# Attention, a Fourier mix and an MLP on one core: where the raw weights' stores, the weight combinations and one activation table load stand in their queues

## The chip, the cores and the metric

The kernel runs on one core of a Trainium2 chip. The metric is the time of one execution on the device in microseconds (us), as the median over several runs. A profiled execution gives a trace: for every instruction its engine, its start and its length. TensorE (PE) multiplies matrices, VectorE (DVE), ScalarE (ACT) and GpSimd (POOL) work elementwise, and SyncE (SP) issues most of the DMA transfers. Each engine takes the instructions of its own queue in order.

## The reference

Eight batches of 576 tokens with 8 heads of 64 columns. The attention has no product of q with k: k is normalized by a softmax over the tokens, q by a softmax over a head's columns, and each head needs only a 64x64 product of k and v. What follows is a Fourier mix over tokens and columns, a layer norm, and an MLP 512 to 2048 to 512.

```python
q_s = np.exp(q - np.max(q, axis=-1, keepdims=True))
q_s = q_s / (np.sum(q_s, axis=-1, keepdims=True) + 1e-09)
k_s = np.exp(k - np.max(k, axis=2, keepdims=True))
k_s = k_s / (np.sum(k_s, axis=2, keepdims=True) + 1e-09)
kv = np.einsum('bhsd,bhse->bhde', k_s, v)
x = np.einsum('bhsd,bhde->bhse', q_s, kv)     # then (B, S, H*D): columns h*64+d
mixed = np.real(np.fft.fft(np.fft.fft(x, axis=1), axis=2))
u = x + mixed
un = (u - mean(u)) / np.sqrt(var(u) + 1e-06)  # over the last axis
out = u + np.maximum(un @ w_ch1, 0.0) @ w_ch2
```

The MLP's weights are handed over as 64-bit words: the core gets them as pairs of 32-bit integers and makes 32-bit floats of them itself.

## The kernel before, in words

**Groups and batches.** The MLP works on groups of 512 tokens. Groups 0 to 6 are the batches 0 to 6 without the 64 tokens of each that a Fourier symmetry folds differently; group 8 holds these tokens of all batches ("xs", "shared"); group 7 comes last. While one group's MLP fills PE, the attention, the transform and the norm of the next batch are interleaved with it, step by step. The order in which steps are written is a request: a scheduler below it arranges the instructions of each engine by priority and by what they wait for, and after that each queue is strictly in order.

**Attention.** `attention` makes items of a batch: 4 of k (two heads' columns each), 4 of q, and for even batches one of the folded tokens ("t"). Each item passes stages, pipelined one step apart: load (SP, L437 for k, L499 for q), exponential (DVE maximum, ACT exponential L457 for k, L521 for q, DVE sums up to L526), transposes on PE (L467, L532) with their copies on ACT (L468, into `ks`), and the matmuls with v (L484), whose result DVE scales into `kvr` (L487), or with kvr (L564).

**Fourier mix.** `transform` first folds x into sums and differences (`tokens_folded`, `columns_folded`, `by_frequency`, `columns_again`; tiles "eo", L603 to L625), one step each for batches from 1 on, then five blocks of small matmuls (L655, L658). `front` splits this into 9 steps for b > 0 with `late`, and `mix_own` (L678) follows with the second Fourier matrix and adds to x.

**Norm.** `norm` takes statistics of four tiles (`stats`), ACT the root (L730), DVE the reciprocal; `normal` scales on ACT (L744, groups from 1 on), `turn` transposes on PE (L750) and copies on ACT into `unT` (L754), and `combine` inside it forms the combinations of unT for Strassen (L348 to L351). ACT evaluates a function from a table set that must be loaded: the exponential and the root are in different sets, so the trace shows a load at the root (L730) and one at the next batch's first exponential (L457).

**The MLP.** Group 0 is multiplied plainly (`plain`): up has 16 steps f of 4 matmuls (L780) with a Relu (L782), down 64 steps in the order DOWN (L789, sum L794, then the store of the output; tiles of one half go by way of a buffer in DRAM, "mirror"). The groups after it use Strassen's scheme with 7 products of half-size blocks: up L850, down L886. Its 7 combinations of the weights come as a stream from DRAM (`w1s`, `w2s`) through four buffers in `big` (`load`, L384 to L395).

**Weights.** `round_blocks` fetches 32 blocks of words (L302 to L315, 512 KB each) into 11 places, and `convert` turns each into floats in `w1sb` and `w2sb`: ACT L329, DVE L330 and L331, ACT L334, POOL L335. A place that is free again takes a later fetch. During group 0's up, blocks up to 27 are converted; the last four, `rest`, follow during group 0's down. During that down, `combine(l, p)` also makes the combinations for layer l and pair p (POOL L341, DVE L343, for the second layer L348 to L351), and stores them beside the plain quarters from which they are made: L376 and L377 on SP store raw quarters, L379 to L382 the computed ones. `rest` and `combine` are one list, spread evenly over the first 60 of the 64 down steps:

```python
other = rest + combine
for i in range(len(down)):
    down[i]()
    for step in other[i * len(other) // 60:(i + 1) * len(other) // 60]:
        step()
```

The first three loads of the stream stand between the two layers' combinations, a fourth (18, which is pair 3's first-layer block) at their end.

**Holding.** `hold` takes the tiles in which batch 1's k and q will land, and `free(f)`, called after each up step f, gives them back by a tiny DVE copy that depends on the Relu of step f (k at f = 12, q at f = 14). That keeps batch 1's loads behind the words on the DMA engines. At f = 15 it copies one column of each of the 16 blocks of `w1sb` onto itself. Such a copy makes later readers of those columns wait for it: the first column of each block lies in the first half of its 512 columns, so the quarters 0 and 2 of the layer are concerned, and the odd quarters are not. The last k, v and q tiles of batch 1 land in the buffer of unT ("spare"), which is free when the last up matmul has read it.

Of the kernel before, what the change touches and what calls it, by code (L numbers as in the profile page):

```python
# [40 lines left out]
F32 = mybir.dt.float32  # L41
I32, U32 = mybir.dt.int32, mybir.dt.uint32
ACT = mybir.ActivationFunctionType
# [3 lines left out]
P = 128  # L47
# [5 lines left out]
HD = D // 2  # L53
# [9 lines left out]
NF = FF // P  # L63
# [59 lines left out]
class _Block:  # L123
# [129 lines left out]
    def hold(self):  # L253


        held = {12: [("k", S, 2)] * 2, 14: [("q", D, 3)] * 3}
        for f, some in held.items():
            for i, (tag, n, bufs) in enumerate(some):
                t = self.work.tile([P, n], F32, tag=tag, name=tag, bufs=bufs)
                self.nc.gpsimd.memset(t[0:1, 0:1], 0.0)  # L260
                some[i] = t[0:1, 0:1]

        def free(f):
            copy = self.nc.vector.tensor_copy
            for t in held.get(f, ()):
                copy(t, self.h0[0:1, f, 0:1])
            if f == NF - 1:
                copy(self.w1sb[0:1, :, 0:1], self.w1sb[0:1, :, 0:1])
        return free

    def shared(self, a, b):
# [318 lines left out]
    def transform(self, b):  # L590


        nc, V, G = self.nc, self.nc.vector, self.nc.gpsimd
        Z = self.work.tile([P, KT, HD], F32, tag="Z", name="Z", bufs=1)
        self.Z[b] = Z
        x = {(c, u): self.xpart(b, c, u) for c in range(2) for u in range(2)}
        eo = {}

        def tokens_folded(some=range(4)):
            for i in some:  # L600
                e, op = ((V if b == 0 else G), ALU.add) if i < 2 else (V, ALU.subtract)
                eo[i] = self.halves()
                e.tensor_tensor(out=eo[i][:, 0:D], in0=x[i % 2, 0], in1=x[i % 2, 1], op=op)  # L603

        def columns_folded(some=range(4)):
            for i in some:
                e, op = ((V if b == 0 else G), ALU.add) if i < 2 else (V, ALU.subtract)
                t = eo[i]
                e.tensor_tensor(out=t[:, 1:HD], in0=t[:, 1:HD], in1=t[:, D - 1:HD:-1], op=op)
                if b == 0:  # L610
                    self.warm(t[:, 0:HD], 2)

        def by_frequency(some=range(4)):

            for i in some:
                e, op = ((G, ALU.add), (G, ALU.subtract), (V, ALU.add), (V, ALU.subtract))[i]
                one, two = eo[i // 2 * 2], eo[i // 2 * 2 + 1]
                (V if b == 0 else e).tensor_tensor(out=eo[i][:, NN:], in0=one[:, 0:NN], in1=two[:, 0:NN], op=op)

        def columns_again(some=(2, 3, 0, 1)):  # L620

            for i in some:
                t, y = eo[i], eo[i][:, NN:]
                V.tensor_tensor(out=t[:, 0:QD], in0=y[:, 0:QD], in1=y[:, HD:QD:-1], op=ALU.subtract)
                V.tensor_tensor(out=y[:, 0:QD], in0=y[:, 0:QD], in1=y[:, HD:QD:-1], op=ALU.add)  # L625

        def at_first():

            for some in ((2, 3), (0, 1)):
                for f in (tokens_folded, columns_folded, by_frequency, columns_again):  # L630
                    f(some)

            t = self.small.tile([P, 1], F32, tag="root", name="root", bufs=1)
            V.tensor_scalar(out=t[:], in0=eo[1][:, NN:NN + 1], scalar1=0.0, scalar2=None, op0=ALU.mult)
            nc.scalar.activation(t[:], t[:], ACT.Sqrt)
            self.wait_for(eo[1][:, NN:], [self.raws[i] for i in range(4)])

        def block(k):


            g = self.live["g", b]
            sines = k in (2, 3)
            own = slice(*{0: (NN, NN + QD), 4: (NN + QD, NN + QD + 1), 1: (0, QD), 2: (NN + 1, NN + QD + 1),
                          3: (1, QD)}[k])
            tail = slice(*{0: (0, QD), 4: (QD, QD + 1), 1: (NN, NN + QD), 2: (1, QD + 1), 3: (NN + 1, NN + QD)}[k])
            n = own.stop - own.start
            if k == KT:

                own, tail = slice(own.start, own.start + P), slice(tail.start, tail.start + P)
            full = self.acc((own.stop - own.start, 512))  # L650
            pz = full[0:n]
            f = sines * NM
            for odd, at, size in ((1, 0, MO), (0, MO, ME)):
                t = eo[3 - odd if sines else odd]
                nc.tensor.matmul(full[:, at:at + size], lhsT=t[:, own], rhs=self.ft[:, f + at:f + at + size], start=at == 0,  # L655
                                 stop=False, skip_group_check=True)
            f += 2 * NM
            nc.tensor.matmul(full[:, 0:NM], lhsT=g[:, tail], rhs=self.ft[:, f:f + NM], start=False, stop=True,  # L658
                             skip_group_check=True)
            z, zt = (self.Zr[0:1], self.ZTr[0:1]) if k == KT else (Z[0:n, k, :], self.ZT[0:n, k, :])  # L660
            nc.scalar.copy(paired(z), interleaved(pz[:, NT - 1:NT - 1 + 2 * ME])[:, 0:P, :])

            at = W * (b % 2)
            nc.scalar.mul(paired(zt[:, at:at + Q]), interleaved(pz[:, 0:2 * MO])[:, 0:NT - 1, ::-1],
                          -1.0 if sines else 1.0)
            nc.scalar.copy(paired(zt[:, at + Q:at + W]), interleaved(pz[:, 0:2 * ME])[:, NT - 2::-1, ::-1])

        folds = [tokens_folded, columns_folded, by_frequency, columns_again] if b else [at_first]
        return folds + [lambda k=k: block(k) for k in (2, 3, 0, 1, 4)]

    def second(self, z, zr, add):

# [43 lines left out]
    def norm(self, g):  # L716

        nc, V = self.nc, self.nc.vector
# [9 lines left out]

        def scales(s):
            nc.scalar.activation(std[:, s], mv[:, s, 1], ACT.Sqrt, bias=self.eps[:, 0:1])  # L730
            V.reciprocal(std[:, s], std[:, s])
            V.scalar_tensor_tensor(out=mv[:, s, 0], in0=mv[:, s, 0], scalar=-1.0, in1=std[:, s], op0=ALU.mult,
                                   op1=ALU.mult)
# [211 lines left out]
def kernel(ctx: ExitStack, tc: tile.TileContext, q, kT, v, w1, w2, ft,  # L945
# [4 lines left out]
    def front(b, loads=None):  # L950

        first = blk.attention(b, loads)
        steps = late(lambda: blk.transform(b), 9 if b else 6)
        mixes = [lambda c=c: blk.mix_own(b, c) for c in range(2)]
        if b % 2:

            mixes.insert(0 if b == B - 1 else 2, lambda: blk.mix_shared(b // 2))
        return first, steps + mixes

    def late(make, n):  # L960

        box = []

        def run(i):
            if not box:
                box.extend(make())
            box[i]()

        return [lambda i=i: run(i) for i in range(n)]
# [33 lines left out]
    for order, g in enumerate(groups):  # L1003
        loads = [] if g == 0 else None
        one, two = front(order + 1, loads) if order + 1 < B else (blk.later, [])
        if g == 0:
            up, down = blk.plain(0, nexts.pop(0))

            round_blocks(range(4))
            n = 2 * NF - 8  # L1010
            for f in range(NF):
                up[f]()
                free(f)
                round_blocks(range(4 + n * f // NF, 4 + n * (f + 1) // NF))
            rest = [lambda i=i: round_blocks([i]) for i in range(4 + n, 2 * NF)]
            combine = [lambda l=l, p=p: blk.combine(l, p) for l in range(2) for p in range(NP)]
            combine[NP:NP] = [lambda i=i: blk.load(15 + i) for i in range(3)]
            combine.append(lambda: blk.load(18))
            for step in loads:
                step()  # L1020

            side = one + two + norm(1)
            gaps = [2] + [2] * 4 + [8] + [2] * (len(one) - 6) + [3] * 5 + [1] * 4 + [2] * (len(two) - 9) + [1] * 7
            other = rest + combine
            at = 0
            for i in range(len(down)):
                down[i]()
                for step in other[i * len(other) // 60:(i + 1) * len(other) // 60]:
                    step()
                while side and at + gaps[0] <= i:  # L1030
                    at += gaps.pop(0)
                    side.pop(0)()
            for step in side:
                step()
            continue

        jobs, down = blk.up(order, nexts.pop(g)), blk.down(g, order)

        merged(flat(jobs), one)
        merged(down, two + (norm(groups[order + 1]) if order < B else []))  # L1040
# [52 lines left out]
```

## Time and profile before

| what | value |
|---|---|
| median of 3 runs | 1142.52 us (1142.41 to 1143.66) |
| profiled execution, its own time | 1142.0 us |
| its span, first to last instruction | 1140.2 us |
| granted TensorE clock | 0.996 |
| DMA moved | 193.79 MB, mean 170 GB/s |
| ACT_TABLE_LOAD, each | 1.28 us |

The profile's page gives the busy time of each engine over the span, the span in 40 slices, and groups of instructions. A slice is 28.5 us here; the digits are tenths of busy time, and the row of GB/s is what the DMA engines moved:

```profile
PE   5899999989999999999999999999999999999997
...
DVE  6785756488324833384435643683344352203201
ACT  6495423274124513371226322641233142201200
...
DMA  9377784463346534554356436543453344444451
```

The first two slices are the attention of batch 0, while the words are still on their way; group 0's MLP takes slices 3 to 7, and from about 200 us on each group's Strassen products run with the next batch beside them.

Two more kinds of view are used below. A timeline lists one engine's instructions in the order of time: start and length in us, the engine, the line, the instruction with its tiles, and how many alike stand in a row; a square bracket at the end gives how long the engine had been idle and what released it. A table by stage gives, for each stretch of time, the length, then the busy us of PE, PE's weight loads, DVE, ACT and POOL (number of instructions in brackets), the clock, the share of DMA and GB/s.

### The profile page before, as it was taken

The numbers are of one execution on the slowest core, as the hardware profiler recorded it, in microseconds if no ns is written. First come the engines' busy times: TensorE is split into PE (matmuls) and PEld (weight loads), VectorE is DVE, ScalarE is ACT, GpSimd is POOL, SyncE is SP. The second block draws the span as 40 slices with busy tenths as digits, with TensorE's granted clock in tenths as the row PEclk, the third lists the DMA queues.
The fourth block names the chain that finished last, engine by engine and source line by source line (L and its number), as shares of the span: only waits on it lengthen the run. The fifth ranks groups of instructions, "written<-read, shape, count | busy, mean of one in ns | idle before, by whom it ended". The sixth has DMA issues, their size and how long they took to land.

```text
span 1140.2 us, 14639 instructions
## 1 busy us (share of the span) xinstructions
PE 1098.6 (96%) x5472; PEld 919.1 (81%) x5472; DVE 543.4 (48%) x1110; ACT 397.7 (35%) x956; POOL 332.5 (29%) x302
## 2 busy tenths in 40 slices
PE   5899999989999999999999999999999999999997
PEld 4644556878888988888889888888889888888886
DVE  6785756488324833384435643683344352203201
ACT  6495423274124513371226322641233142201200
POOL 2075541245012600324024402260034213302320
PEclk9999999999999999999999999999999999999999
DMA  9377784463346534554356436543453344444451
GB/s 310 120 258 243 258 279 148 149 213 140 122 150 206 202 111 143 183 195 154 124 176 213 148 113 190 195 172 107 143 191 148 114 163 148 185 139 154 150 185 55
DMA packets 92549, 193.79 MB, mean 170 GB/s; under 512 B 23088, under 2 KB 59696, under 8 KB 85312
## 3 DMA queue, kind: packets, MB, share of 16 engines
q1 hardware_dynamic: 90680, 191.82, 49.5%
q10 hardware_dynamic: 1800, 1.05, 0.3%
q8 instruction: 43, 0.70, 0.2%
q14 instruction: 26, 0.21, 0.1%
HBM read 168.72 MB, written 28.31 MB: 173 GB/s over the span
## 4 chain that ended last, share of the span: by engine, by line
PE 79%; DVE 11%; ACT 4%; DMA 2%; issue 2%; POOL 1%; SPq 0%; ACTq 0%; POOLq 0%; DVEq 0%
PE bb L850 14%; PE bb L886 13%; PE bc L886 10%; PE bc L850 9%; PE ba L850 9%; PE ba L886 8%; PE acc L484 3%; PE acc L564 2%; PE bc L789 2%; PE acc L655 2%; PE acc L658 2%; PE acc L678 1%; PE tr L750 1%; PE tr L532 1%; PE tr L467 1%
## 5 line engine op out<-in xcount | busy, mean ns | idle before, releaser
L850 PE MATMUL bb<-unT,big 128*128 128x256 f32 x768 | 187.9, 381 | 0.3 <-DVE u L822 0.3
L886 PE MATMUL bb<-big 128*128 128x256 f32 x768 | 172.8, 379 | 0.0
L850 PEld LDWEIGHTS bb<-unT,big 128*128 128x128 f32 x768 | 142.8, 190 | 23.8 <-DVE u L818 3.4
L886 PEld LDWEIGHTS bb<-big 128*128 128x128 f32 x768 | 145.1, 190 | 20.1
L341 POOL TENSOR_TENSOR big<-big 128x512 f32<-128x512 f32 (+1 forms) x38 | 45.1, 1187 | 309.5 <-ACT big L862 305.6
L850 PE MATMUL bc<-unT,big 128*128 128x256 f32 x512 | 125.3, 379 | 0.0
L850 PE MATMUL ba<-unT,big 128*128 128x256 f32 x512 | 124.3, 379 | 0.0
L862 ACT ACTIVATE big<-big 128x512 f32<-128x512 f32 x96 | 60.2, 628 | 171.3 <-DVE big L861 171.0
L886 PE MATMUL bc<-big 128*128 128x256 f32 x512 | 116.5, 379 | 0.5 <-DVE x L903 0.5
L886 PE MATMUL ba<-big 128*128 128x256 f32 x512 | 114.1, 379 | 0.0
L886 PEld LDWEIGHTS bc<-big 128*128 128x128 f32 x512 | 95.9, 190 | 14.1 <-DVE x L903 0.9
L886 PEld LDWEIGHTS ba<-big 128*128 128x128 f32 x512 | 95.9, 190 | 12.3
L850 PEld LDWEIGHTS bc<-unT,big 128*128 128x128 f32 x512 | 95.5, 190 | 12.5
L850 PEld LDWEIGHTS ba<-unT,big 128*128 128x128 f32 x512 | 95.0, 190 | 11.7
L822 DVE TENSOR_TENSOR u<-bb,s 128x512 f32<-128x512 f32 x40 | 27.6, 689 | 134.8 <-PE bb L886 79.1
L521 ACT ACTIVATE q<-q,qm 128x64 f32<-128x64 f32 x240 | 61.5, 337 | 10.2 <-DVE qm L519 9.4
L349 POOL TENSOR_TENSOR unT<-unT 128x512 f32<-128x512 f32 x8 | 14.2, 1773 | 172.9 <-DVE unT L348 172.9
L818 DVE TENSOR_TENSOR u<-bb,s 128x512 f32<-128x512 f32 x40 | 27.6, 690 | 76.8 <-PE bb L850 38.1
L898 POOL TENSOR_TENSOR x<-x,u 128x512 f32<-128x512 f32 x14 | 17.7, 1267 | 148.2 <-DVE u L822 118.0
L861 DVE TENSOR_TENSOR big<-bc,u 128x512 f32<-128x512 f32 x64 | 44.1, 688 | 26.1 <-PE bc L850 25.3
L814 ACT COPY s<-ba 128x512 f32<-128x512 f32 x40 | 23.4, 584 | 89.4 <-PE ba L886 45.5
L754 ACT COPY unT<-tr 128x512 f32<-128x512 f32 x36 | 20.6, 585 | 86.5 <-PE tr L750 86.0
(221 smaller groups left out, 1656.7 us busy)
## 6 DMA issues: line engine op xcount, KB each, us to landing
big<-w1s SPq DMA_DIRECT2D x64, 896.0 KB
big<-w2s SPq DMA_DIRECT2D x56, 1024.0 KB
big<-in_w_dram SPq DMA_DIRECT2D x21, 512.0 KB
k<-in_kT_dram SPq DMA_DIRECT2D x26, 288.0 KB
q<-in_q_dram SPq DMA_DIRECT2D x27, 256.0 KB
v<-in_v_dram SPq DMA_DIRECT2D x26, 256.0 KB
words<-in_w_dram SPq DMA_DIRECT2D x11, 512.0 KB
w2s<-big SPq DMA_DIRECT2D x8, 512.0 KB
```

Of the source, the lines that this page charges most:

```text
L341: e1.tensor_tensor(out=to(4), in0=at(2), in1=at(3), op=ALU.add)
L484: nc.tensor.matmul(pk, lhsT=ks[:, c, :], rhs=v[:, c, :], start=(c == 0), stop=(c == NC - 1))
L521: nc.scalar.activation(heads[:, h, :], heads[:, h, :], ACT.Exp, bias=m[:, h:h + 1])
L564: nc.tensor.matmul(px[:, r * P:(r + 1) * P], lhsT=qT[:, r, :], rhs=self.kvr[b % 2][:, r, :], start=True, stop=True)
L655: nc.tensor.matmul(full[:, at:at + size], lhsT=t[:, own], rhs=self.ft[:, f + at:f + at + size], start=at == 0, stop=False, skip_group_chec ...
L814: nc.scalar.copy(temp("s1"), box["ba"][:])
L818: V.tensor_tensor(out=temp("u2"), in0=box["bb"][:], in1=box["s1"][:], op=ALU.add)
L822: V.tensor_tensor(out=temp("u3"), in0=box["bb"][:], in1=box["s1"][:], op=ALU.add)
L850: nc.tensor.matmul(bank()[:, i, :], lhsT=w[:, WA_AT[m], k * P:(k + 1) * P], rhs=unT[:, B_AT[m], k, :], start=first and i == 0 and k == 0, ...
L861: V.tensor_tensor(out=hp(i), in0=bank[:], in1=u[:], op=ALU.add)
L862: nc.scalar.activation(hp(i), hp(i), ACT.Relu)
L886: nc.tensor.matmul(bank()[:, i, :], lhsT=h[p][:, A_AT[m], i * P:(i + 1) * P], rhs=w[:, p, :], start=first and i == 0 and p == 0, stop=p == ...
```

## The change

Four places are edited.

- `free` at f = 15 copies two strided views onto themselves: of all 16 blocks of `w1sb` the columns 0 and 256, and of the first 12 blocks of `w2sb` (blocks 16 to 27 of the words) the same two. So the odd quarters are concerned too, and so are the raw stores of the second layer that read these blocks.
- `rest` and `combine` are two lists: `rest` has one step at down steps 0, 3, 6 and 9, and `combine` is spread over the 50 down steps from 12 on.
- In `norm`, groups from 1 on get one exponential of a single column after the root, into a small tile of its own that nobody reads. It needs the exponential's table set, which is therefore loaded there.
- `transform` has one empty step between the folds and the blocks for batches from 2 on, and `front` asks for 10 steps there instead of 9.

```diff
@@ free
             if f == NF - 1:
-                copy(self.w1sb[0:1, :, 0:1], self.w1sb[0:1, :, 0:1])
+                for w in (self.w1sb[0:1, :, ::HD], self.w2sb[0:1, 0:NF - 4, ::HD]):
+                    copy(w, w)
@@ transform
-        return folds + [lambda k=k: block(k) for k in (2, 3, 0, 1, 4)]
+        return folds + [lambda: None] * (b > 1) + [lambda k=k: block(k) for k in (2, 3, 0, 1, 4)]
@@ norm, scales
             nc.scalar.activation(std[:, s], mv[:, s, 1], ACT.Sqrt, bias=self.eps[:, 0:1])
+            if g > 0:
+                t = self.small.tile([P, 1], F32, tag="root", name="root", bufs=1)
+                nc.scalar.activation(t[:], std[:, 0:1], ACT.Exp)
             V.reciprocal(std[:, s], std[:, s])
@@ front
-        steps = late(lambda: blk.transform(b), 9 if b else 6)
+        steps = late(lambda: blk.transform(b), (6, 9, 10)[min(b, 2)])
@@ group 0's down
-            other = rest + combine
             at = 0
             for i in range(len(down)):
                 down[i]()
-                for step in other[i * len(other) // 60:(i + 1) * len(other) // 60]:
+                for step in rest[i // 3:i // 3 + 1] if i % 3 == 0 else []:
+                    step()
+                j = max(0, i - 12)
+                for step in combine[j * len(combine) // 50:(j + 1) * len(combine) // 50 if i >= 12 else 0]:
                     step()
```

## Prediction

> **What bounds the kernel now.** I read the page first, then the stages, then every wait of the TensorE in order of time, then what the releasing engine did. The page says PE is busy 1098.6 of 1140.2 us, so all waits of PE together are 41.6 us, and only those that the change can reach are worth counting.
>
> ```profile
> PE 1098.6 (96%) x5472; PEld 919.1 (81%) x5472; DVE 543.4 (48%) x1110; ACT 397.7 (35%) x956; POOL 332.5 (29%) x302
> ```
>
> The stages show where they lie (the column after the length is PE busy): the first 60 us (about 21 us idle) and the end (8 us after 1100) are not touched; 100 to 150 has 4.2 us, 225 to 275 has 3.8 us.
>
> ```profile
> 100.00:125.00 25.00, 23.93 (x59) 10.62 (x59) 9.34 (x22) 9.03 (x16) 10.04 (x13) 1.00 0.78 248
> 125.00:150.00 25.00, 21.89 (x103) 14.13 (x104) 22.30 (x57) 15.60 (x49) 10.05 (x12) 1.00 0.78 295
> ...
> 225.00:250.00 25.00, 22.57 (x127) 18.83 (x125) 18.08 (x42) 17.74 (x50) 6.85 (x7) 1.00 0.51 166
> 250.00:275.00 25.00, 23.68 (x132) 20.83 (x131) 22.53 (x37) 16.57 (x50) 13.79 (x10) 1.00 0.49 191
> ```
>
> PE's timeline gives each wait (in brackets: us waited and the releaser). After 275 us there are only 3.8 us of them before the last stage.
>
> ```profile
> 99.97 3.67 PE L780 MATMUL bc<-unT,big 128*128 128x512 f32 x8 [0.94 <-ACT big L782]
> ...
> 126.63 1.38 PE L484 MATMUL acc<-v,ks 128*128 128x128 f32 x10 [2.69 <-ACT ks L468]
> ...
> 147.60 0.49 PE L564 MATMUL acc<-kvr,qT 128*128 128x128 f32 x2 [1.48 <-DVE kvr L487]
> ...
> 232.14 0.66 PE L467 MATMUL tr<-ident,k 128*128 128x128 f32 x4 [1.47 <-ACT k L457]
> ...
> 254.11 0.66 PE L532 MATMUL tr<-ident,q 128*128 128x128 f32 x4 [1.32 <-DVE q L526]
> ...
> 478.28 0.66 PE L467 MATMUL tr<-ident,k 128*128 128x128 f32 x4 [1.04 <-ACT k L457]
> 479.67 1.38 PE L484 MATMUL acc<-v,ks 128*128 128x128 f32 x10 [0.19 <-ACT ks L468]
> ```
>
> The pair at 478/479 returns at 721.96/723.35. ACT shows why: the table load stands between the last Relu and the first exponential, on the path.
>
> ```profile
> 476.06 1.28 ACT L457 ACT_TABLE_LOAD   x1
> 477.36 0.78 ACT L457 ACTIVATE k<-k,km 128x576 f32<-128x576 f32 x1
> ```
>
> The wait at 126.63 is a chain through SP's queue: k loads, ACT's exponentials of k, the Relu of f=14 behind them (114.60), the q loads that it frees, the spare loads behind those, their maximum on DVE (124.46) and exponential (125.24), and then the copy of ks that PE waits for.
>
> ```profile
> 100.62 1.81 SPq L377 DMA_DIRECT2D w2s<-big  x3
> ...
> 107.91 0.83 SPq L437 DMA_DIRECT2D k<-in_kT_dram  x2
> ...
> 115.38 2.73 SPq L499 DMA_DIRECT2D q<-in_q_dram  x3
> ...
> 118.67 0.39 SPq L437 DMA_DIRECT2D spare<-in_kT_dram  x1
> ```
>
> **What the Trainium skill says.** "ScalarE: Activation LUTs", What ACT_TABLE_LOAD costs: about 1283 ns for the load, plus a drain of about 1380 ns, for every switch of set. The load agrees (1283 ns, 7 times at L457 and 7 at L730); no drain is seen, the exponential starts 1.30 us after its load does. I use 1.28. "PSUM — Partial Sum Buffer", Engine vs sequencer instructions: ScalarE, VectorE and GpSimd queues are strict FIFO, and matmuls start in program order. The trace agrees: the Relu of f=14 (L782) stood behind two exponentials until 114.60. So the order of each queue decides, and I compared the orders of both kernels' instructions.
>
> **The change, part by part** (line numbers of before).
>
> *Raw stores held.* Before, 8 stores of the w1 quarter (L377, 128 KB) go out from 79.81, and w2's raw stores stand between the last word fetches. In the new order the w1 ones come after the spare loads, one ahead of each combination's; of w2's raw stores one pair stays between fetches 29 and 30, and 13 stand behind fetch 31 and ahead of the k loads. Two waits are new. First, DVE's 24-element copy on w2sb waits for POOL's conversion 25 (done 97.62); behind it on DVE are conversions 26 and 27, which ran from 95.35, so they start 2.3 us late, POOL's follow at 99.7 and 101.0 instead of 97.67 and 98.95, and fetches 30 and 31 go out at about 101.0 and 102.3 (before 98.99 and about 100.2). They then have less ahead of them, so I let them land as before. Second, 13 stores at 0.43 to 0.60 us each (L376 and L377 rows) need 5.6 to 7.8 us of SP, and the third from last waits for conversion 30: k loads at about 109 instead of 107.91. Passing that on with DMA's lighter backlog: Relu of f=14 +0.6, q loads +0.6, spare loads 119.3, their landing 124.4 instead of 123.8 (from the DMA semaphores in the trace). But before, DVE's maximum did not start at the landing: a combination waiting for POOL (L343) held it until 124.46. With that moved behind, the maximum starts at 124.4 again, so the end of the wait stays at 126.6. The 0.94 at 99.97 lies before it on PE; removed or not, it is made up in this wait. Sum: 0, from -1.0 to +1.5, with a tail taken up below.
>
> *Combinations behind the keys.* Up to the last kvr (L487, 146.97) DVE runs without a gap from 126.4. In the new order the same span holds as many half-size combinations (14), but conversion 30 (L330 and L331, 1.38 us) has moved ahead of it. Part is lost to waits for the stores, so the kvr comes 0.9 us earlier and the wait of 1.48 is 0.6: gain 0.9 (0 to 1.5). The combinations' DMA waits now stand on DVE ahead of q's sums; I traced the tightest (the store of pair 5's raw halves, out about 138.6, landing about 142, wanted at 145) and charge nothing; the cover is 3 us. Layer two's chain ends near 190 on POOL, wanted at 200; the load of pair 3 moves from 185 behind a mirror store that waits for the last down matmul (201.10): about 203, landing by 209, wanted at 214. Cover 5 us, charged 0.
>
> *Where the batch 1 transposes go.* Before, PE puts down matmuls between them:
>
> ```profile
> 198.88 0.60 PE L750 MATMUL tr<-ident,eo 128*128 128x128 f32 x4
> 199.32 1.02 PE L789 MATMUL bc<-big 128*128 128x512 f32 x2
> 200.18 0.60 PE L750 MATMUL tr<-ident,eo 128*128 128x128 f32 x4
> 200.62 1.89 PE L850 MATMUL ba<-unT,big 128*128 128x256 f32 x8
> ```
>
> In the new order all four tiles stand in a row at the end. With two banks and 0.58 us copies, working on: first transposes at 199.0, copies end at 200.2 and 200.7, the fourth normalization (queued behind them on ACT, 0.75) at 201.4, the third tile's copy at 201.95, and L850 starts then, not at 200.62: loss 1.35 (0.5 to 1.6).
>
> *Exponential table behind the root.* Each of 8 norms gets a load and one small exponential, 1.5 us, on ACT after the root; its normalizations are queued behind and start about 1.0 us later (before: root done 194.23, first one at 194.73). From batch 2 on the new order puts the first transpose up to 7 matmuls (3 us) later, which covers it; ACT is 35% busy. Seven loads leave the exponentials' path. At 478 and 722 the exponential moves 1.28 up, so 1.04 goes; but the matmul between transpose and L484 has moved behind L484, so of 0.19+0.43 about 0.62 is waited: gain 1.23-0.62=0.6 each, 1.2 together (0 to 2). At 232 the transpose itself stands two matmuls (0.86) earlier, so 1.47 becomes about 0.95: gain 0.5. The five transposes of q after it stand 3 to 12 matmuls later; of their waits (0.61+0.30+1.32=2.2) I take 1.6 (0.8 to 2.2).
>
> *The empty step.* For b>1 the blocks move one place down. First blocks of batch 7 stand 4 matmuls (1.7 us) later, so the 0.55 at 889.43 goes, and the transposes at 802.54 (0.39) stand 7 later: gain 0.9 (0.4 to 0.95).
>
> Sum: 0+0.9-1.35+1.2+0.5+1.6+0.9 = 3.75 us. The profiled execution: 1142.0, span 1140.2, 1.8 outside. So 1138.2 for it; the median of the runs shown is 0.5 above it: 1138.8.
>
> **Rivals.**
> A smaller gain: the kvr stays late and the q waits shift with the keys (0.9 and 1.6 gone, a little more lost at 200): 1141.2. For it: DVE is busy 22.3 of 25 us there, and its waits on stores are new. Against: the q transposes do move.
> A larger one: the held stores let the fetches land earlier, and both 0.94 and 2.69 go with the rest kept: 1135.8. For it: the DMA share is 0.78 there. Against: the spare loads cannot start before the first layer has read the buffer (117.2).
> Slower: the k loads are stuck behind w2's raw stores on SP. If fetch 30 and 31 take 6 us, as the third words fetch before did (91.7 to 98.1), instead of 3, conversion 30 is done near 111, and the stores behind it at 0.6 us push the k loads to about 116. Each us is then passed on through Relu, q and spare loads to PE: 7 us against 3.75 gained, near 1146. It decides from 6 us of delay (k loads at 115). For it: SP is in order and nothing else carries k. Against: fewer bytes stand ahead of them.
>
> **How the numbers follow.** A change counts here from 0.2% (2.3 us). Forecast 1138.8: 0.50; smaller 0.25; larger 0.08; slower 0.17. Faster: 0.48 of the first, 0.08, and 0.04 of the smaller: 0.60; same 0.23; slower 0.17. The parts' bounds give 1135.5 to 1142.5 for the first; to leave out no more than two in ten I reach to 1143.5.
>
> **What will show it.** k loads on SP near 109, spare's maximum near 124.4, L484's wait still near 2.7; kvr near 146; L850's first matmul about 1.3 us after the last transpose with a wait on ACT; no table load at L457 after batch 1, and waits at 478 and 722 on L484 instead of L467. I am wrong if k loads come after 112, if DVE waits for w1s stores between 137 and 147, or if L850 waits for the load of pair 3.

## The result, and the profile after

| | median | runs | ratio to before |
|---|---|---|---|
| before, beside the first runs of the change | 1143.09 us | 4 | |
| the change, first runs | 1144.22 us | 4 | 1.0004 (0.9983 to 1.0025) |
| before, beside the later runs | 1142.97 us | 43 | |
| the change again (e7 below) | 1142.51 us | 14 | 0.9996 (0.9986 to 1.0005) |

The change makes no difference that can be measured; the forecast of 1138.8 us was wrong. The profiled execution took 1142.6 us with a span of 1140.8 us at a clock of 0.995, against 1142.0, 1140.2 and 0.996 before.

To see where the time went, I compare the start of the same matmul of the MLP in both traces. The next table is worked out from the two records of PE; a shift above zero is later than before.

| place on PE (time before) | shift in the changed kernel, us | forecast for the stretch | measured for the stretch |
|---|---|---|---|
| group 0, first up matmul (61.0) | +0.15 | | |
| group 0, down matmul 49 (152.3) | +2.90 | -0.9 | +2.75 |
| group 1, first up matmul (200.6) | +4.11 | +1.35 | +1.21 |
| group 1, last up matmul (266.5) | +3.27 | -2.1 | -0.84 |
| group 5, last up matmul (754.0) | +2.53 | -1.2 | -0.74 |
| group 6, last down matmul (935.1); no change after it | +0.97 | -0.9 | -1.56 |

From 200 us on the forecast holds: 3.14 us come back where 4.2 were expected. The loss sits before 152 us. This is the timeline of PE in the changed kernel (start, length, instruction, and in brackets the wait and its releaser); the waits answer to those shown at 99.97, 126.63, 147.60, 478.28 and 479.67 of before:

```profile
103.41 3.67 PE L788 MATMUL ba<-unT,big 128*128 128x512 f32 x8 [0.80 <-ACT big L790]
...
119.28 3.70 PE L797 MATMUL bc<-big 128*128 128x512 f32 x8 [1.34 <-ACT big L790]
...
128.57 2.36 PE L487 MATMUL acc<-v,ks 128*128 128x128 f32 x10 [2.46 <-ACT ks L471]
...
150.50 0.49 PE L567 MATMUL acc<-kvr,qT 128*128 128x128 f32 x2 [0.79 <-DVE kvr L490]
...
203.04 0.66 PE L758 MATMUL tr<-ident,eo 128*128 128x128 f32 x4 [0.24 <-ACT unT L762]
204.24 0.66 PE L758 MATMUL tr<-ident,eo 128*128 128x128 f32 x4 [0.54 <-ACT eo L752]
...
481.89 1.38 PE L487 MATMUL acc<-v,ks 128*128 128x128 f32 x10 [0.62 <-ACT ks L471]
```

The four transposes in a row cost what was said, and the kvr wait (the one at 150.50) halved, though not for the reason given in the forecast, as the experiments show. But the first k times v (L487, L484 before) starts at 128.57, not at 126.6; a new wait of 1.34 on a Relu stands ahead of it. Its ten matmuls then take 2.36 us where they took 1.38. SP's queue shows the cause of the first, the clock that of the second.

SP's timeline (each line is what SP spent on issuing, waits included):

```profile
101.53 1.58 SPq L317 DMA_DIRECT2D words<-in_w_dram  x2
103.15 0.43 SPq L379 DMA_DIRECT2D w2s<-big  x1
...
111.61 0.47 SPq L379 DMA_DIRECT2D w2s<-big  x1
112.17 0.91 SPq L440 DMA_DIRECT2D k<-in_kT_dram  x2
119.43 2.57 SPq L502 DMA_DIRECT2D q<-in_q_dram  x3
...
122.57 0.38 SPq L440 DMA_DIRECT2D spare<-in_kT_dram  x1
```

The k loads go out 4.26 us later than before (107.91), and q and spare loads follow 4 us later. Even an empty SP could not have sent them before 110.5: the k tile is given back only after the Relu of f=12, and that one stood on ACT behind the conversion of late words:

```profile
108.67 0.68 ACT L337 ACTIVATE words<-words 128x512 int32<-128x512 uint32 x1 [1.40 <-DMA words<-in_w_dram]
109.24 0.58 ACT L790 ACTIVATE big<-bc 128x512 f32<-128x512 f32 x1
109.72 0.59 ACT L790 ACTIVATE big<-ba 128x512 f32<-128x512 f32 x1
```

The last of these three is the Relu of f=12; before it ran at 107.11, behind words that had landed by 105.89.

Of the 4.26 us only 1.94 reach the first k times v. The maximum of the spare tile on DVE, which it needs, no longer stands behind a combination that waits for POOL (first two lines, before); it starts as soon as its data have landed (last line, after):

```profile
123.61 0.93 DVE L343 TENSOR_TENSOR big<-big 128x256 f32<-128x256 f32 x1 [2.73 <-POOL big L341]
124.46 0.74 DVE L455 TENSOR_REDUCE km<-spare 128x1 f32<-128x576 f32 x1
...
126.39 0.75 DVE L458 TENSOR_REDUCE km<-spare 128x1 f32<-128x576 f32 x1 [4.13 <-DMA spare<-in_kT_dram]
```

The traces of the experiments below show two effects. In the eight kernels whose first layer's raw stores are not held, the maximum stands behind this combination, and from the k loads to the first k times v it takes 18.2 to 18.7 us (17.5 in e2). In the six that hold them, the maximum starts at the landing, and it takes 16.4 to 16.8 us (17.8 in e7). So the hold shortens this chain by about 2 us, but in the changed kernel the chain starts 4.26 us later.

The clock: two tables by stage, first the kernel before, then the changed one, cut on the grid of the trace's clock record, whose rate changes only there. After the length come PE's busy us; the third number from the end is the clock.

```profile
121.60:125.01 3.41, 2.33 (x10) 1.03 (x8) 1.40 (x2) 0.00 (x0) 2.66 (x4) 1.00 0.99 290
125.01:128.42 3.41, 1.79 (x16) 1.79 (x17) 2.46 (x8) 2.14 (x5) 0.00 (x0) 1.00 1.07 404
128.42:131.84 3.42, 3.42 (x22) 2.46 (x21) 3.36 (x8) 2.25 (x5) 1.34 (x1) 1.00 0.34 130
```

```profile
125.34:128.76 3.42, 0.96 (x3) 0.19 (x2) 1.07 (x3) 1.56 (x4) 2.12 (x3) 1.00 0.96 290
128.76:132.17 3.41, 3.41 (x16) 3.37 (x16) 1.38 (x4) 0.39 (x2) 0.72 (x1) 0.50 1.07 399
```

The changed kernel waits no longer there than the one before (2.46 against 2.69 us), but its wait falls almost whole into one stretch of 3.41 us, and the next stretch runs at half rate: half of 3.41, that is 1.7 us of work, is lost there, and the shift grows from 1.94 at the start of the first k times v to 3.59. Of this 0.69 comes back at the kvr wait, which PE now reaches later; 2.90 are left. Before, the wait was cut in two by the edge at 125.01, and nothing followed.

### The profile page after: what moved, and what is told of

It is laid out like the page before. It is cut to its first block, busy times and chain, and to the rows that moved or that the text cites. A ratio compares the mean times of both kernels' runs of the same rounds, so it can differ in the third digit from the quotient of the medians.

```text
span 1140.8 us, 14655 instructions
## 1 busy us (share of the span) xinstructions
PE 1099.8 (96%) x5472; PEld 920.9 (81%) x5472; DVE 536.1 (47%) x1111; ACT 403.1 (35%) x967; POOL 332.9 (29%) x302
## 4 chain that ended last, share of the span: by engine, by line
PE 84%; DVE 4%; issue 2%; DMA 1%; POOL 1%; ACT 1%; SPq 0%; POOLq 0%; DVEq 0%; ACTq 0%
PE bb L894 15%; PE bb L858 14%; PE bc L894 10%; PE ba L894 10%; PE bc L858 10%; PE ba L858 9%; PE acc L487 2%; PE acc L567 2%; PE bc L797 2%; PE acc L658 2%; PE acc L661 1%; PE acc L682 1%; PE tr L758 1%; PE tr L535 1%; PE tr L470 1%
## 5 line engine op out<-in xcount | busy, mean ns | idle before, releaser
L664 ACT COPY Z<-acc 128x256 f32<-128x256 f32 (+1 forms) x32 | 12.0, 375 | 111.9 <-PE acc L661 111.9
```

## The experiments

Means are over all runs of a kernel, with the runs of before on the same chip; they scatter by about 1.5 us, so that the traces, not the times, tell the places apart. Each kernel has one trace. "Shift" is that of the table above.

**One part alone, and one undone.** e1 is the first edit of the diff on the kernel before, e3 its Exp in `scales`, e2 its two lists; e4 is the changed kernel with the old copy:

```diff
@@ e4: free, on the changed kernel
-                for w in (self.w1sb[0:1, :, ::HD], self.w2sb[0:1, 0:NF - 4, ::HD]):
-                    copy(w, w)
+                copy(self.w1sb[0:1, :, 0:1], self.w1sb[0:1, :, 0:1])
```

e1:

> Only the held raw stores, on the kernel before. Theory A (the early loss comes from the hold: the copy on w2sb delays conversions 26 and 27, fetches 30 and 31 go out at about 101.5 and 103 instead of 99 and 100.2, and some 13 raw stores stand ahead of the k loads): k loads on SP near 112 (107.9 before), the first k-times-v wait (L484) ends near 128.5 instead of 126.6, and the first Strassen matmul starts 2 to 4 us later than the 200.6 of before; time 2 to 4 us above before. Theory B (the early loss comes from the order of the combinations): k loads within 1 us of 107.9, first Strassen matmul within 0.7 us of before, time within 1 us of before. Theory C (the loss is the TensorE clock alone, a half-rate window): k loads and waits as in the changed kernel, but a loss only where the record shows a half-rate window, about 1.7 us for each.

e2:

> Only the combinations behind the keys, on the kernel before. Theory A: k loads within 1 us of 107.9; the kvr wait at 147.6 shrinks by about 0.7 us, first Strassen matmul 0 to 1 us earlier than 200.6; time 0 to 1 us below before. Theory B: conversion 30's ACT step ahead of a Relu delays the chain, first Strassen matmul 2 to 4 us later, time 2 to 4 us above before.

e3:

> Only the exponential behind the root, on the kernel before. Theory A (it is the cause of the four transposes in a row at group 1's start and of the gains after 225 us): four transposes in a row near 199, with about 0.8 to 1.4 us of waits there, then the waits at 232, 478 and 722 shrink by about 0.4 each and the q waits by part; first matmul of the last group's up 0.5 to 2 us earlier than before; time 0.5 to 2 us below before. Theory B (the gains after 225 us come from elsewhere, the exponential is neutral): no shift beyond 0.5 us anywhere, time within 0.5 us of before.

e4:

> The changed kernel without the held raw stores, the free as in the kernel before. Theory A: k loads near 108, no waits on the Relu at 103, 107 and 119, first Strassen matmul near 201 instead of 204.7; time 3 to 5 us below the changed kernel, near 1139.5. Theory B: first Strassen matmul still 3 us or more behind before, time within 1.5 us of the changed kernel. Theory C: time below the changed kernel by the 1.7 us of one half-rate window and no more.

| | ratio to before (51 runs) | k loads on SP | first k times v | shift at group 1's first up matmul | shift at the last group |
|---|---|---|---|---|---|
| e1, hold | 1.0005 (0.9993 to 1.0017), 14 runs | 111.71 | 128.54 | +2.19 | +0.93 |
| e2, behind | 1.0001 (0.9990 to 1.0012), 14 | 111.30 | 128.82 | +3.39 | +2.13 |
| e3, exponential | 0.9983 (0.9974 to 0.9992), 22 | 108.33 | 126.81 | +1.85 | -1.66 |
| e4, without the hold | 0.9989 (0.9975 to 1.0003), 14 | 111.49 | 129.80 | +5.15 | +0.47 |

The traces settle more than the times. In the mean e1 lies 0.4 us and e2 0.2 us above before, e4 1.2 and e3 2.0 us below it; for e1 theory A had 2 to 4 us, for e2 theory B the same, and neither came. Neither theory A nor theory B survives alone. The hold delays the k loads (A), but e4 keeps the delay without it: the two lists do the same by themselves (B). Together they do not add up, because both act on the same queue. Theory C, the clock alone, fails with e1: its first k times v is 1.9 us late at the end of a wait for ks, so that PE's clock does not set it, and no half-rate stretch follows. e3 did what was forecast of it: late gains of 3.5 us, a loss of 1.2 at the transposes. In e4 a half-rate stretch at the up matmuls' start (58.3 to 65.1 us) made PE 1.9 us late; since PE then waits 4.27 us ahead of the first k times v, it is open how much of this is in the shift of 5.15. Another 1.7 us arose behind the first k times v; e1's half-rate stretch lay at 120.65 and was made up by a shorter wait (0.54 us at 128.54).

**Which half of the second part.** The two lists move two things: `rest` from down steps 2, 4, 7, 9 to 0, 3, 6, 9, and the combinations by two steps and more. e5 moves only the first, e6 only the second:

```diff
@@ e5: rest as changed, combinations as before
+                for step in rest[i // 3:i // 3 + 1] if i % 3 == 0 else []:
+                    step()
+                j = max(0, i * 24 // 60 - 4), max(0, (i + 1) * 24 // 60 - 4)
+                for step in combine[j[0]:j[1]]:
+                    step()
@@ e6: rest as before, combinations as changed
+                for step in rest[i * 2 // 5:(i + 1) * 2 // 5]:
+                    step()
+                j = max(0, i - 12)
+                for step in combine[j * len(combine) // 50:(j + 1) * len(combine) // 50 if i >= 12 else 0]:
+                    step()
```

> On the kernel before, only the steps of rest moved (conversions 28 to 31 at down steps 0, 3, 6, 9 instead of 2, 4, 7, 9), the combinations where they were. Theory A (the early step of rest alone pulls conversion 30 ahead of the Relus and its raw store ahead of the k loads): k loads on SP at 111 to 111.6 behind a store that waits for POOL's conversion 30 near 109.8, first k-times-v matmuls at 128.3 to 129 instead of 126.6; mean time of the runs 0 to 1 us above before. Theory B (the combinations' place is what delays the k loads): k loads within 0.7 us of 107.9, first k-times-v matmuls near 126.6.

> On the kernel before, only the combinations moved (spread over the 50 down steps from 12 on, rest at 2, 4, 7, 9 as before). Theory A: k loads within 0.7 us of 107.9, first k-times-v matmuls at 126.6, the kvr wait of 1.48 at 147.6 falls to 0.7 or less; mean time 0.3 to 1.5 us below before. Theory B: k loads at 111 or later and first k-times-v matmuls at 128.3 or later.

e5: 1.0004 (0.9996 to 1.0013), 13 runs, mean 0.65 us above before; e6: 0.9995 (0.9988 to 1.0003), 13 runs, mean 0.67 below. e5 on SP and, below it, on POOL:

```profile
107.31 0.44 SPq L376 DMA_DIRECT2D w2s<-big  x1
109.73 0.36 SPq L377 DMA_DIRECT2D w2s<-big  x1
110.14 0.47 SPq L376 DMA_DIRECT2D w2s<-big  x1
110.70 0.89 SPq L437 DMA_DIRECT2D k<-in_kT_dram  x2
```

```profile
108.42 1.29 POOL L335 TENSOR_TENSOR big<-big,words 128x512 int32<-128x512 int32 x1 [1.68 <-DVE big L331]
```

SP stands from 107.75 to 109.73 until POOL has finished conversion 30 at 109.71: a store of its result has moved ahead of the k loads. In the kernel before this conversion is made after 126 us. So conversion 30, moved by one down step (from 7 to 6), costs the k loads 2.8 us; theory A holds. In e6 the k loads go out at 109.40, which is 1.5 us later than before; but its up matmuls were 1.1 us late already, after a half-rate stretch at their start, and the shift stays at 1.1 to 1.3 us from there to the end. The gain at kvr that I expected there did not come. Here is its wait, and below it that of e3, which moves no combination at all:

```profile
148.81 0.49 PE L564 MATMUL acc<-kvr,qT 128*128 128x128 f32 x2 [1.50 <-DVE kvr L487]
...
148.24 0.49 PE L564 MATMUL acc<-kvr,qT 128*128 128x128 f32 x2 [0.27 <-DVE kvr L487]
```

Over all 14 traces the wait goes with the clock and not with the combinations. Where a half-rate stretch covers the first k times v or begins behind it (the changed kernel, e2 to e5, e7, e9), PE comes later to kvr and waits 0.82 us or less; in the other seven it waits 1.48 to 2.00. From the start of the first k times v to the end of the kvr wait it takes 20.97 us before, 20.99 in e6 and 21.93 in the changed kernel: moving the combinations made kvr nowhere earlier.

**The changed kernel again, and with its wait filled.** e8 puts six matmuls that nobody reads in front of the first k times v:

```diff
@@ e8: k_times_v, on the changed kernel
         _, v, rec, ks = self.live.pop(it)
+        if it[1:] == (1, 0):
+            junk = self.acc((P, HD))
+            for _ in range(6):
+                nc.tensor.matmul(junk, lhsT=self.ident[:], rhs=self.ft[:, 0:HD], start=True, stop=True)
```

> The changed kernel itself, for more runs of it beside those of before. Half-rate theory (a window of 3.4 us in which TensorE idles for most of it is followed by one at half rate, which costs 1.7 us where TensorE is the bound; the window's place is chance): times between 1140 and 1147 that fall as the mean clock rises, about 0.8 us for each 0.001; mean 0 to 1 us above before. Rival (the spread has another cause): no relation of time and clock.

> The changed kernel with 6 matmuls of 256 columns whose result nobody reads ahead of the first k times v of batch 1, where TensorE stood idle for 2.46 us. Half-rate theory: they fill about 2.2 us of that wait, no half-rate window follows between 125 and 135 us, the mean clock rises by about 0.001 and the mean time falls by 0.5 to 1.7 us against the changed kernel. Rival (the windows do not depend on this idle time, or the matmuls only lengthen the path): half-rate windows there as before, mean time the same or up to 2 us above the changed kernel.

e7: 0.9996 (0.9986 to 1.0005), mean 0.1 us below before; its runs go from 1146.05 us at a mean clock of 0.992 to 1140.73 at 0.998. The 51 runs of before beside e1 to e4 say the same: 1142.0 us on average at 0.997 (14 runs), 1143.3 at 0.995 (9), 1144.4 at 0.994 (8), so about 0.8 us for each 0.001. e8 missed: 1.0020 (1.0007 to 1.0032), mean 2.2 us above e7, at the same mean clock (0.9951 and 0.9952). In its profiled execution the wait is filled and no half-rate stretch follows, but the k times v behind it starts at 129.75, though the copy of ks that it needs was done at 129.22. Why e8 loses 2 us in the mean is not settled; the filling is no remedy.

**What helps, kept.** e9 keeps the exponential for groups from 2 on, the empty step and e6's lists; e10 is the hold for the first layer alone, on the kernel before; e11 the empty step alone; e12 is e9 with e10:

```diff
@@ e9: scales
+            if g > 1:
+                t = self.small.tile([P, 1], F32, tag="root", name="root", bufs=1)
+                nc.scalar.activation(t[:], std[:, 0:1], ACT.Exp)
@@ e10, e12: free
-                copy(self.w1sb[0:1, :, 0:1], self.w1sb[0:1, :, 0:1])
+                copy(self.w1sb[0:1, :, ::HD], self.w1sb[0:1, :, ::HD])
```

> What helped, kept together: the exponential behind the root for groups from 2 on only, the empty step, the combinations spread from down step 12 on; the free and the steps of rest as in the kernel before. Theory A (the losses were the hold, the early step of rest and the four transposes in a row that the exponential of group 1 makes): k loads within 1 us of 107.9, transposes of batch 1 between down matmuls without a wait near 200, no table load at the exponentials of batches 3 and later; mean of the runs 2.5 to 4.5 us below before, below each part alone. Rival (the gains share one slack and do not add up): 1 to 2 us below before, like the exponential alone.

> On the kernel before, the hold for the first layer's raw stores alone (columns 0 and 256 of w1sb, nothing of w2sb). Theory A (it is the copy on w2sb that costs: DVE waits there for POOL ahead of conversions 26 and 27, and the second layer's stores gather ahead of the k loads): k loads on SP at 108 or before, the Relu waits at 103 and 119 gone, first k-times-v matmuls at 126.6 or before, mean within 0.7 us of before or up to 1 below. Rival (holding the first layer's stores costs by itself, since they crowd in later): first k-times-v matmuls at 128 or later, mean 0.3 to 1.5 us above before.

> On the kernel before, the empty step alone. Theory A (it moves the first blocks behind their folds): the waits of 0.55 at 889 and 0.39 at 802 go, no new one comes; mean 0.4 to 1.0 us below before. Rival (the 0.39 at 802 belongs to the order of the norm and not to the step, or another wait comes in its place): 0 to 0.5 us below before, 0.39 at 802 still there.

> The kept parts of e9 with the hold of the first layer's raw stores alone (columns 0 and 256 of w1sb) as in e10. Theory A (independent places: the hold shortens the wait of the first k times v and spares the half-rate window behind it, the exponential, the step and the combinations work elsewhere): mean 4 to 5.5 us below before, mean clock 0.996 or above, wait ahead of the first k times v below 1 us. Rival (the same slack is counted twice): 3 to 3.7 us below before, no better than e9.

| | median (before beside it) | ratio | mean against before |
|---|---|---|---|
| e9, kept parts | 1139.73 (1142.73) | 0.9970 (0.9960 to 0.9981), 15 runs | -3.0 us |
| e10, first layer's hold | 1140.59 (1142.73) | 0.9981 (0.9973 to 0.9988), 21 | -2.35 us |
| e11, empty step | 1142.14 (1142.73) | 0.9995 (0.9985 to 1.0005), 13 | -0.7 us |
| e12, all of them | 1137.86 (1142.66) | 0.9961 (0.9946 to 0.9976), 6 | -4.1 us |

e12 is faster than both kernels. In e9 the transposes of batch 1 stand between down matmuls again and nothing waits there, so they were the doing of group 1's exponential. In e11 the waits at 802 and 889 are gone, and its shift falls there by 0.37 and 0.80 us; the small wait that before has at 770 (0.16) is still there. e10 shows what the first edit is worth without the copy on `w2sb`; PE's timeline:

```profile
126.63 1.38 PE L487 MATMUL acc<-v,ks 128*128 128x128 f32 x10 [0.58 <-ACT ks L471]
```

Its up matmuls began 1.42 us later than before in this execution, its k loads went out at 110.03, 2.1 us later (not at 108, as expected, and waits of 0.50 and 0.92 on a Relu stayed), and still the first k times v starts at the same 126.63. e11, without the hold, began as late (1.39) and starts it 1.09 late, so the hold is worth about 1.1 us at this place. Most of the wait is gone, and with it the reason for a half-rate stretch in this trace. Whether it spares the other executions half-rate stretches is not shown: the mean clock is 0.9963 against 0.9951 of before, but 0.9961 in e6 too, where a wait of 2.79 stands; and the weak relation of time and clock (correlation -0.30 against -0.85) is weaker still in e11 (-0.06), with a wait of 2.38. The rival for e10, that the held stores cost later, is out. Another 1.0 us is gained between 200 and 266 us, where the waits at q's transposes and products shrink from 2.23 to 1.06 us, as they do in e1; which of DVE's moved instructions does that I have not followed.

Between "adds up" and "counted twice" e12 lies in the middle: 4.1 us where e9 and e10 make 5.4, with an interval of 2.7 to 6.2 us from six runs, which holds both the 5.4 and the 3.0 of e9 alone. The wait ahead of its first k times v is 0.37 us, as expected; its mean clock is 0.9955 and not 0.996 or above. Its kvr wait grew to 2.00 us, and a half-rate stretch followed there in the profiled execution:

```profile
146.02:149.44 3.42, 1.42 (x11) 1.18 (x10) 3.34 (x11) 0.00 (x0) 1.06 (x1) 1.00 0.68 256
149.44:152.85 3.41, 3.41 (x8) 1.76 (x7) 2.03 (x4) 1.17 (x2) 1.56 (x2) 0.50 1.02 353
```

## Why the prediction was wrong, by its own steps

- **"Raw stores held. Sum: 0"** is the step that failed: where it put nothing, 1.8 us are lost between 61 us and the first k times v (the shift goes from 0.15 to 1.94). It gave k loads at about 109, and said that k loads after 112 would disprove it; they went out at 112.17. Two of its terms were too small. The 13 stores were priced at 5.6 to 7.8 us of SP; their issues took 7.1, within this range, but with the gaps between them (0.45 and 0.80 us the largest) they filled 8.9, from 103.15 to 112.08; what SP waited for in the gaps I leave open. And "I let them land as before" was wrong for the last words: ACT got them at 108.67 instead of 105.89, and the Relus that give the k tiles back stand behind them on ACT. In e1 this edit alone moves the first k times v by 1.9 us. The other half of the step was right: the maximum that starts at its landing does absorb a delay. In e10, with k loads at 110.03, the maximum starts at 124.45 and the wait ends at 126.63, as this step had it.
- **The copy on w2sb** was seen and traced to fetches 30 and 31 at 101.0 and 102.3 (101.53 to 103.1 measured), but given no price. e10 shows that without it the same edit gains 2.35 us. So what failed is the price of this copy, and not the idea of the hold.
- **"Combinations behind the keys: gain 0.9"** failed too, and the kvr wait hides it. The wait fell from 1.48 to 0.79, close to the 0.6 of the forecast, but by luck: PE came later to kvr, since the half-rate stretch had held it up. kvr itself came 0.96 us later after the first k times v, not 0.9 earlier, and e6, with the combinations moved and no such stretch there, gains nothing (20.99 us against 20.97). The same edit also moves conversion 30 ahead of the k loads, which I priced as 1.38 us of DVE work and as one store among 13; alone it delays them by 2.8 us (e5). The two delays overlap, so that the changed kernel pays once.
- **The half-rate stretch** is in no term: 1.7 us in the profiled execution, of which 0.7 came back at kvr. I took the unchanged end of a wait for an unchanged cost. With 1.8 us from the late k loads and about 1.0 from here the stretch up to 152 us has its 2.75.
- **Transposes in a row, loss 1.35**: 1.21 measured, and the waits of 0.24 and 0.54 are where they were expected.
- **Exponential behind the root**: the mechanism was right, though six loads and not seven leave the exponentials' path (batch 1's stays, at 115.83). ACT's timeline has the load where it was said, 1.28 us and one small exponential ahead of the normalizations:

```profile
196.83 0.30 ACT L734 ACTIVATE std<-mv,eps 128x4 f32<-128x4 f32 x1 [1.74 <-DVE mv L731]
197.15 1.28 ACT L738 ACT_TABLE_LOAD   x1
198.44 0.20 ACT L738 ACTIVATE root<-std 128x1 f32<-128x1 f32 x1
199.15 2.22 ACT L752 ACTIVATE eo<-x,mv,std 128x512 f32<-128x512 f32 x3 [0.50 <-DVE mv L740]
```

  The sizes were off: at 478 and 722 the waits stand on L487 with 0.62 us, as forecast, but new waits on q's sums follow (0.68 us at 500.37, 0.67 at 743.35), and 0.49 us came at each place instead of 0.6. e3 gains 2.0 us over the stretch where the changed kernel gains 0.74. Of this difference 0.8 us lie at 750, where the changed kernel waits 0.52 us on DVE (before 0.28, e3 not at all); some 0.2 us each near 340 and by 600 come with the empty step, since e11 loses them too. For 232 to 261 us the terms 0.5 and 1.6 were too high; 0.84 came, since a wait of 1.66 us at 258.49 remains.
- **Empty step, gain 0.9**: in e11, which has it alone, the last stretch of the table gives 1.17 us. The 0.39 at 802 and the 0.55 at 889 are gone, with a little more around them than was counted. The 1.56 of the changed kernel is not all the step's: 0.40 of it lies at 770, where e3 gains the same and e11 nothing.
- **The slower rival** had the right place and the right mechanism, k loads behind raw stores, but its point of decision was 115 us. At 112.17 it had gone more than half of the way, and with the half-rate stretch that cancels the gains; a delay of this middle size was in none of the cases. That each us is passed on to PE was wrong: 4.26 us at the k loads were 1.94 at the first k times v.

## What to carry to other kernels

Before a store is moved ahead of a load in one queue, ask which engine finishes its data last, and write that time down as the earliest start of everything behind it; "so many stores of so many us" is only the lower bound. A step that is moved by one place can carry its DMAs ahead of a critical load, so compare the queue of the DMA issuer first and the engines afterwards. Judge each part of a change alone: here one line gained 2.4 us with half of its operand and nothing with the whole. And where a wait shrinks, ask whether what it waits for came earlier or the waiting engine came later.

## What the runs showed of the hardware

The TensorE clock falls to half rate for one stretch of 3.41 us, or two, on a grid whose place differs from run to run. I took PE's busy time in every full-rate stretch of this grid from 20 to 200 us in the 14 profiles. With 1.42 us or less, the next stretch was at half rate (21 of 21 cases); from 1.46 to 1.77 us it was so in 5 of 13; above that never. The stretch at 146.02 of e12 above is at the edge, and this one of e8 is just beyond it:

```profile
118.54:121.96 3.42, 1.46 (x4) 0.75 (x5) 1.28 (x9) 2.39 (x6) 1.03 (x2) 1.00 0.10 23
121.96:125.37 3.41, 3.41 (x13) 1.69 (x12) 1.48 (x2) 0.00 (x0) 2.79 (x4) 1.00 1.01 315
```

The Trainium skill, "TensorE: Matmul & The Clock Gate", What's actually happening, has the free-running window of 3413 ns, and these traces agree with it; it names a whole idle window as the condition, and here the measurement decides: a stretch that was idle for 58% was always enough, and some with half. A stretch already at half rate stayed there after 1.87 us of work (e7, from 129.24). So a wait of 2 to 3.4 us costs itself or, by chance of its place on the grid, up to 1.7 us more, less what a later wait gives back (0.7 in the changed kernel; in e12, where none follows, the shift grows by 1.5 and stays). The relation of time and clock above suggests that this makes much of the scatter of the runs; removing such a wait can be worth more than its length.
